# A fused spectral mixer and SwiGLU kernel: row scales stored from GpSimd, and transfers given other places in the order

## The chip, the cores and the metric

The kernel runs on one core of a Trainium2 chip. A core has five engines with a queue of its own each: TensorE (PE in the profile, with weight loads as PEld), VectorE (DVE), ScalarE (ACT), GpSimd (POOL) and SyncE (SP). Each works its queue strictly in order and waits where an instruction's input or buffer isn't ready. PE writes to PSUM banks, DVE and ACT read them. Transfers between HBM and SBUF are issued by SP or by GpSimd and carried out by DMA engines that they share. The metric is the device time of one execution in microseconds; lower is better.

## The reference, cut to what matters

There are 8 sequences of 3008 rows with 256 channels. Each is filtered in the frequency domain, and every row of the result then goes through an RMS norm and a SwiGLU feed-forward layer without biases.

```python
X = np.fft.rfft(x, axis=1)                       # x: 8 x 3008 x 256
Y = X * (filt_r + 1j * filt_i)[None]
y = np.fft.irfft(Y, n=3008, axis=1)              # -> 24064 rows of 256
rms = np.sqrt(np.mean(y * y, axis=-1, keepdims=True) + 1e-06)
xn = y / rms * rms_g
g = xn @ w_gate                                  # 256 x 1536
out = (g / (1 + np.exp(-g)) * (xn @ w_val)) @ w_out
```

## The kernel before

The transform of 3008 = 64 x 47 points is done as matmuls in four stages for each sequence. Stage A (`a_unit`, 12 a sequence) multiplies x by the 64-point table, copies the PSUM result to a tile `t1` on ACT or DVE, and stores each `t1` (3 units, a chunk) to the HBM buffer `z_tmp` (`z_store`). A bounce load (`t2_load`, 4 a sequence) brings it back in another order. Stage B (`b_unit`, 16 a sequence) does the second step, and multiplies by the filter (`s1`, `s2`). For sequences 2 to 7 this is done by DVE and a sum on GpSimd (`swap_unit`, L277); for sequence 1 the two products are made by DVE, or, for some units, by GpSimd, and then ACT first copies the PSUM bank to a tile `v`[...]. `v` is taken from the pool `yp`, which has three buffers and serves the norm's tiles `y` as well. `bi_unit` transforms back some slots later (a lag of 4 for sequence 1, 5 for sequence 2, 8 after that), `g_store` stores to `g_tmp`, `t4_load` brings it back, and `n_unit` does the last step and gives `y` and its squares. `negate` turns the sign of a quarter of the filter for the later sequences, on GpSimd, during stage B of sequence 1.

Sequence 0 has no other work to run beside. It stays on the chip through transposes, in a part ahead of the main loop; the filter, the weights (`w_load`, three parts) and x are loaded there.

The norm of a tile of 512 rows, called (b, m), takes: `q_unit`, a sum of squares on PE, `u` on DVE and the power -0.5 on GpSimd, which gives the row scales `rho`; `rho_move`, which stores `rho` to the HBM buffer `r_tmp` (2 KB); `rho_load`, which reads it back to all partitions as `rb` (256 KB, on SP); and `xn_unit`, the product of `y` and `rb` on GpSimd. The first two tiles of sequence 0 take another way, over PE (`scale_split`, `scale_apply`).

The main loop has 576 items (b, m, jt): 8 sequences, 6 tiles of rows, 12 blocks of 128 hidden columns. Item i does the gate and value matmuls (`gv`: `pg`, `pv`, L421), SiLU on ACT (L425), the product on DVE (L426), and two items later the output matmuls (`down`, L438). Everything else is put in by hand: `at(slot, fn, ...)` adds a call behind the item of that number, and the lists `a_at`, `b_at`, `n_at` and the offsets at L713 to L759 say which. The order of calls is the order on each engine. So a slot says behind what an instruction stands in its engine's queue, and not when it runs: a GpSimd or SP instruction starts as soon as all ahead of it on that queue are done and its own waits are over.

Three more things matter. GpSimd's transfers use eight semaphores in turn, so that one waits for the landing of the one eight before it; SP's likewise. Stage A uses PSUM bank 3 for units copied by DVE and bank 0 for those copied by ACT (`bank(3 if on_dve else 0, ...)`, L202); bank 3 is also stage B's and bank 0 that of `bi_unit` and `n_unit`. And `t1` has two buffers, so chunk c + 2 of stage A waits until chunk c has landed in `z_tmp`; x (`xp`) has four.

Of the kernel before, what the change touches and what calls it, by code (L numbers as in the profile page):

```python
# [20 lines left out]
P = 128  # L21
# [13 lines left out]
NXC = H // XC  # L35
# [87 lines left out]
def kernel(  # L123
# [11 lines left out]
    nc = tc.nc  # L135
# [7 lines left out]
    r_d = nc.dram_tensor("r_tmp", (B, 6, P * 4), FP32, kind="Internal").ap()  # L143
# [36 lines left out]
    def x_load(b, c):  # L180
        t = xp.tile([P, XC, D], FP16, tag="xc", name="xc")
        last = c == NXC - 1
        if last:
            nc.gpsimd.memset(t[64:P, XC - 1, :], 0.0)
        rows = x[b].rearrange("(n2 n1) d -> n2 n1 d", n1=N1)
        for h in range(2):
            w = XC - 1 if (last and h) else XC
            lo = h * H + c * XC
            nc.gpsimd.dma_start(t[h * 64:h * 64 + 64, 0:w, :], rows[:, lo:lo + w, :])  # L189
        st[b]["x"][c] = t  # L190

    def bank(i, name):

        pool, tag = ((psM, "mx"), (psG, "pg"), (psV, "pv"), (psB, "mb"), (psO, "po1"), (psO, "po0"))[i]
        return pool.tile([P, 512], FP32, tag=tag, name=name)
# [26 lines left out]
    def filt(k, n):  # L222
        c, r = divmod(k, KC)
        return fr[c][:, r:r + n, :], fi[c][:, r:r + n, :]
# [4 lines left out]
    def b_unit(b, i):  # L229
        if b:  # L230
            ps = bank(3, "psb")
        else:
            ps = bank((0, 3, 4, 5)[i % 4], "psb")
        ps = ps.rearrange("p (a d) -> p a d", a=2)
        for u in range(2):
            k = 2 * i + u
            if b:
                w, t = late_p["wb"], st[b]["t2"][k // KC][:, k % KC, :]
            else:
                w, t = wbp, st[0]["t2"][k // 4][:, k % 4, :]  # L240
            nc.tensor.matmul(ps[:, u, :], w[:, k, :], t, start=True, stop=True)  # L241
        f1, f2 = filt(2 * i, 2)
        if b:
            s1 = late_p["sp"].tile([P, 2, D], FP16, tag="s1", name="s1")
            s2 = late_p["sp"].tile([P, 2, D], FP16, tag="s2", name="s2")
            if b > 1:
                nc.vector.tensor_tensor(out=s1, in0=ps, in1=f1, op=ALU.mult)  # L247
                st[b]["s"][i] = (s1, s2, ps, f2)
                return
        elif i % 2:  # L250
            s1 = hp.tile([P, 512], FP16, tag="sg", name="sg").rearrange("p (a d) -> p a d", a=2)
            s2 = hhs[(i // 2) % 4].rearrange("p (a d) -> p a d", a=2)
        else:
            ss = xnp.tile([P, 2, 512], FP16, tag="xn", name="ss")
            s1, s2 = (ss[:, e, :].rearrange("p (a d) -> p a d", a=2) for e in range(2))
        eng = nc.vector
        if (i % 3 == 2) if b else (i in (4, 8, 11)):
            eng = nc.gpsimd
            v = yp.tile([P, 2, 512], FP32, tag="y", name="v")
            v = v[:, 0, :].rearrange("p (a d) -> p a d", a=2)  # L260
            nc.scalar.activation(out=v, in_=ps, func=AXT.Copy)
            ps = v
        eng.tensor_tensor(out=s1, in0=ps, in1=f1, op=ALU.mult)
        eng.tensor_tensor(out=s2, in0=ps, in1=f2, op=ALU.mult)  # L264
        st[b]["s"][i] = (s1, s2)
# [41 lines left out]
    def nq(b, m):  # L307
        return 3 if (m == 5 and b % 2 == 0) else 4
# [38 lines left out]

    def rho_move(b, m):
        n = nq(b, m)
        nc.sync.dma_start(r_d[b, m, 0:n * P].rearrange("(p q) -> p q", q=n),  # L350
                          st[b]["u"].pop(m)[:, 0:n])

    def rho_load(b, m):
# [122 lines left out]
    def f_dup(c):  # L476
        for t, a, e in ((fr[c], HALF, 0), (fi[c], 0, HALF)):
            if c == 2 or (c == 3 and a):
                nc.scalar.activation(out=t[a:a + HALF], in_=t[e:e + HALF], func=AXT.Copy)
            else:  # L480
                nc.gpsimd.tensor_copy(out=t[a:a + HALF], in_=t[e:e + HALF])
# [98 lines left out]
    def w_load(q):  # L580
        cols = ts(q, DFF // 3)
        for src, dst in ((moe_w_gate, wg), (moe_w_val, wv)):
            nc.gpsimd.dma_start(dst[:, :, cols], src.rearrange("(dt p) j -> p dt j", p=P)[:, :, cols])
        nc.gpsimd.dma_start(wo[:, ts(q, JT // 3), :],
                            moe_w_out.rearrange("(jt p) d -> p jt d", p=P)[:, ts(q, JT // 3), :])

    with tc.manual_schedule():
# [49 lines left out]
        for i in range(16):  # L637
            if i == 7:
                f_dup(3)
            b_unit(0, i)  # L640
            if i % 2 and i >= 5:
                bit_unit(i - 5)
                bit_unit(i - 4)
            if i == 4:
                f_dup(2)
            if i == 11:
                for q in range(3):
                    w_load(q)
                x_load(1, 0)
                x_load(1, 1)  # L650
        for i in range(12, 16):
            bit_unit(i)
        t2_unit(0, 1)
# [9 lines left out]
        scale_apply(0, 3)  # L663
        t2_unit(4, 0)
        t2_unit(5, 0)
        x_load(1, 2)
        x_load(1, 3)

        def open_late():
            nc.sync.dma_start(bass.AP(tensor=g_d.tensor, offset=g_d.offset + (H - 1) * D,  # L670
# [18 lines left out]
        def at(slot, fn, *a):  # L689
            todo = (late if fn == q_unit else plan).setdefault(slot, [])  # L690
            if fn in (sq_unit, swap_unit):
                todo.insert(0, (fn, a))
            else:
                todo.append((fn, a))

        def norm_plan(b, m, s0, s1, r):
            for dh in range(2):
                at((s0, s1)[dh], n_unit, b, m, dh)
                at((s0, s1)[dh] + 1, sq_unit, b, m, dh)
            for d, fn in zip(r, (q_unit, rho_move, rho_load, xn_unit)):  # L700
                at(s1 + d, fn, b, m)
# [11 lines left out]
        for b in range(1, B):  # L713
            t = (b - 1) * 72
            on_dve = ()
            n_at = [t + 51 + 8 * m for m in range(6)]
            n_step, lag, t4_at = 4, 8, t + 46
            a_at = [t - 103 + 12 * (i // 2) + 4 * (i % 2) for i in range(12)]
            b_at = [t - 26 + 4 * i for i in range(16)]
            if b == 1:  # L720
                a_at = [8, 9, 9, 10, 10, 11, 11, 12, 12, 13, 13, 14]
                on_dve = (2, 4, 6, 8, 10)
                b_at = [22 + 7 * i // 4 for i in range(16)]
                lag, t4_at = 4, 55
                n_at, n_step = [58, 62, 74, 86, 95, 107], 3
            elif b == 2:
                a_at = [51, 52, 53, 53, 54, 55, 55, 56, 56, 57, 57, 58]
                on_dve = (0, 2, 3, 5, 6, 8, 10, 11)
                b_at = [71 + 3 * i for i in range(16)]
                lag, t4_at = 5, 123  # L730
                n_at = [127 + 8 * m for m in range(6)]
            elif b == 3:
                a_at = [72, 73, 80, 81, 83, 84, 92, 93, 101, 102, 104, 105]
            for i in range(12):
                at(a_at[i], a_unit, b, i, i in on_dve)
                if i % 3 == 2:
                    at(a_at[i] + 1, z_store, b, i // 3)
            for c in range(4):
                at(b_at[0] - 4 + c // (1 + (b == 1)) if c < 3 else b_at[4] + 1, t2_load, b, c)
            for i in range(16):  # L740
                s0 = b_at[i]
                at(s0, b_unit, b, i)
                if b > 1:
                    at(s0 + 1, swap_unit, b, i, 0)
                    at(s0 + 2, swap_unit, b, i, 1)
                at(s0 + lag, bi_unit, b, i)
                if b == 1 and i in (3, 7, 11, 15):
                    at(s0 + 2, negate, i // 4, 0, 8)
                if i % 2 == 1:
                    at(s0 + lag + 1, g_store, b, i // 2)  # L750
            if b + 1 < B:
                for c in range(NXC):
                    at(a_at[3 * c + 2] + 2, x_load, b + 1, c)
            for c in range(4):
                at(t4_at + (c // 2 * 2 if b == 1 else c), t4_load, b, c)
            for m in range(6):
                step = 2 if b == 1 and m < 2 else n_step
                norm_plan(b, m, n_at[m], n_at[m] + step,
                          (2, 4, 6, 10) if b > 1 else (2, 3, 4, 7))  # L759
# [45 lines left out]
```

## Time and profile before

| | before |
|---|---|
| median of 8 runs | 939.6 us (937.61 to 945.3) |
| the profiled execution | 938.85 us, span 937.1 us |
| PE busy | 892.6 us (95%) |
| DVE, ACT, POOL busy | 673.6 (72%), 620.2 (66%), 390.4 us (42%) |
| mean granted TensorE clock | 0.979 |
| DMA moved | 101.17 MB, mean 108 GB/s |
| SP's queue | 34.3% of 16 engines' span |
| GpSimd's queue | 11.3% of 16 engines' span |

Times are in microseconds from the first instruction. "Busy" adds an engine's instructions; matmuls overlap one another, so that a busy PE may still be slower than it could be. In a group or a timeline row the engine, the source line, `out<-in` by the program's names and the shapes are given; what stands in brackets is the idle time just before and what ended it. A row of the waits reads: engine, line, what it waited for, microseconds in total, times, longest. `SPq` is SP issuing a transfer. The granted clock is 1.0 at full speed.

### The profile page before, as it was taken

The numbers are of one execution on the slowest core, as the hardware profiler recorded it, in microseconds if no ns is written. First come the engines' busy times: TensorE is split into PE (matmuls) and PEld (weight loads), VectorE is DVE, ScalarE is ACT, GpSimd is POOL, SyncE is SP. The second block draws the span as 40 slices with busy tenths as digits, with TensorE's granted clock in tenths as the row PEclk, the third lists the DMA queues.
The fourth block names the chain that finished last, engine by engine and source line by source line (L and its number), as shares of the span: only waits on it lengthen the run. The fifth ranks groups of instructions, "written<-read, shape, count | busy, mean of one in ns | idle before, by whom it ended". The sixth has DMA issues, their size and how long they took to land.

```text
span 937.1 us, 17504 instructions
## 1 busy us (share of the span) xinstructions
PE 892.6 (95%) x6321; PEld 564.1 (60%) x6321; DVE 673.6 (72%) x1068; ACT 620.2 (66%) x1049; POOL 390.4 (42%) x315
## 2 busy tenths in 40 slices
PE   8779898899989999999999999999999999999997
PEld 5555455556546666666666666666666666666554
DVE  7746456578878777787868778788878888555554
ACT  7647455567747776687667776687656775576543
POOL 7923486245532554145532554044522554033200
PEclk9779799999999999999999999999999999999999
DMA  8588433736536444643565434543353323332201
GB/s 200 88 154 188 90 83 79 205 88 146 131 98 168 96 97 113 184 97 98 96 187 116 97 83 112 171 94 83 80 172 82 64 63 71 100 71 49 57 24 45
DMA packets 85074, 101.17 MB, mean 108 GB/s; under 512 B 13296, under 2 KB 61616, under 8 KB 84604
## 3 DMA queue, kind: packets, MB, share of 16 engines
q1 hardware_dynamic: 76044, 83.81, 34.3%
q0 software_dynamic: 8944, 16.26, 11.3%
q8 instruction: 49, 0.80, 0.4%
q14 instruction: 37, 0.30, 0.1%
HBM read 67.93 MB, written 46.79 MB: 122 GB/s over the span
## 4 chain that ended last, share of the span: by engine, by line
PE 74%; DMA 10%; DVE 5%; POOL 4%; issue 2%; ACT 2%; SPq 1%; POOLq 0%; DVEq 0%; ACTq 0%
PE po L438 22%; PE pg L421 22%; PE pv L421 21%; PE psi L286 2%; PE psb L241 2%; DVE hh L426 2%; PE psn L318 2%; DMA fr<-in_filt_r_dram 2%; DMA t<-g_tmp 2%; PE psa L204 2%; DVE o L444 1%; DMA t<-z_tmp 1%; DMA z_tmp<-t 1%; DMA g_tmp<-t 1%; POOL xn L405 1%
## 5 line engine op out<-in xcount | busy, mean ns | idle before, releaser
L426 DVE TENSOR_TENSOR hh<-pv,sg 128x512 f16<-128x512 f32 (+1 forms) x576 | 391.7, 680 | 223.1 <-ACT sg L425 104.8
L425 ACT ACTIVATE sg<-pg 128x512 f16<-128x512 f32 (+1 forms) x576 | 338.9, 588 | 253.7 <-PE pg L421 243.4
L438 PE MATMUL po<-wo,hh 128*128 128x256 f16 x2256 | 346.3, 274 | 2.7 <-DVE o L444 0.6
L421 PE MATMUL pg<-xn,wg 128*128 128x512 f16 (+1 forms) x1152 | 340.5, 377 | 0.4 <-POOL xn L405 0.4
L421 PE MATMUL pv<-xn,wv 128*128 128x512 f16 (+1 forms) x1152 | 340.3, 377 | 0.0
L438 PEld LDWEIGHTS <-hh 128*128 128x128 f16 x2256 | 217.8, 98 | 106.9 <-issue 10.9
L277 POOL TENSOR_TENSOR s<-s,s 128x512 f16<-128x512 f16 x96 | 110.7, 1153 | 326.2 <-DVE s L274 254.8
L421 PEld LDWEIGHTS <-wv 128*128 128x128 f16 x1152 | 113.3, 98 | 133.1 <-issue 3.9
L405 POOL TENSOR_TENSOR xn<-y,rb 128x1024 f16<-128x1024 f32 (+1 forms) x46 | 128.9, 2803 | 60.9 <-DMA rb<-r_tmp 49.0
L274 DVE TENSOR_TENSOR s<-psb,fi 64x512 f16<-64x512 f32 x192 | 132.2, 688 | 5.9
L421 PEld LDWEIGHTS <-wg 128*128 128x128 f16 x1152 | 109.4, 98 | 13.7 <-issue 1.4
L345 POOL TENSOR_TENSOR rho<-u,mhalf 128x4 f32<-128x4 f32 (+1 forms) x48 | 48.5, 1011 | 73.3 <-DVE u L343 66.8
L291 ACT ACTIVATE t<-psi 96x512 f16<-96x512 f32 x112 | 66.4, 593 | 12.3 <-PE psi L286 7.3
L324 ACT ACTIVATE y<-psn,gsb 128x512 f32<-128x512 f32 (+1 forms) x94 | 63.8, 679 | 10.6 <-PE psn L318 3.9
L247 DVE TENSOR_TENSOR s<-psb,fr 128x512 f16<-128x512 f32 x96 | 65.3, 680 | 4.2 <-PE psb L241 4.2
L330 ACT ACTIVATE sq<-psn 128x512 f16<-128x512 f32 (+1 forms) x94 | 54.8, 582 | 0.0
L241 PE MATMUL psb<-t,wb 96*128 96x256 f16 x224 | 43.9, 277 | 11.3 <-DMA t<-z_tmp 9.3
L209 ACT ACTIVATE t<-psa 128x512 f16<-128x512 f32 x71 | 42.4, 597 | 10.4 <-PE psa L204 4.5
L286 PE MATMUL psi<-s,wi 128*128 128x256 f16 x248 | 46.0, 275 | 1.1 <-POOL s L264 1.0
L318 PEld LDWEIGHTS <-t 128*128 128x128 f16 x368 | 28.9, 99 | 22.9 <-issue 2.8
L286 PEld LDWEIGHTS <-wi 128*128 128x128 f16 x248 | 24.4, 99 | 27.3 <-issue 2.4
L189 POOL DMA_DIRECT2D xc<-in_x_dram x64 | 35.2, 555 | 13.1 <-PE psa L204 8.2
(96 smaller groups left out, 475.3 us busy)
## 6 DMA issues: line engine op xcount, KB each, us to landing
out_dram<-o SPq DMA_DIRECT2D x84, 256.0 KB
xc<-in_x_dram POOLq DMA_DIRECT2D x56, 192.0 KB, 6.3
rb<-r_tmp SPq DMA_DIRECT2D x42, 256.0 KB
z_tmp<-t SPq DMA_DIRECT2D x28, 384.0 KB
t<-z_tmp SPq DMA_DIRECT2D x28, 384.0 KB
g_tmp<-t SPq DMA_DIRECT2D x56, 192.0 KB
t<-g_tmp SPq DMA_DIRECT2D x21, 384.0 KB
out_dram<-o SPq DMA_DIRECT2D x12, 192.0 KB
```

The lines of the kernel that those rows point to most:

```text
L241: nc.tensor.matmul(ps[:, u, :], w[:, k, :], t, start=True, stop=True)
L247: nc.vector.tensor_tensor(out=s1, in0=ps, in1=f1, op=ALU.mult)
L274: nc.vector.tensor_tensor(out=s2[a], in0=ps[e], in1=f2[e], op=ALU.mult)
L277: nc.gpsimd.tensor_tensor(out=s, in0=s1, in1=s2, op=ALU.add)
L286: nc.tensor.matmul(ps[:, u, :], wi_at(q, 2 * i + u), ss[q][:, u, :], start=(q == 0), stop=(q == n - 1))
L291: nc.scalar.activation(out=st[b]["t3"][c][:, 2 * r:2 * r + 2, :], in_=ps[0:KR], func=AXT.Copy)
L324: nc.scalar.activation(out=y[:, dh, 0:w], in_=ps[:, 0:w], func=AXT.Identity, scale=gsb[:, dh:dh + 1])
L405: nc.gpsimd.tensor_tensor(out=xv, in0=yv, in1=rv.unsqueeze(1).to_broadcast([P, 2, n, P]), op=ALU.mult)
L421: nc.tensor.matmul(ps[:, 0:w], wt[:, dt_, ts(jt, P)], xn[:, dt_, 0:w], start=(dt_ == 0), stop=(dt_ == 1))
L425: nc.scalar.activation(out=sg[:, 0:w], in_=pg[:, 0:w], func=AXT.Silu)
L426: nc.vector.tensor_tensor(out=hh[:, 0:w], in0=pv[:, 0:w], in1=sg[:, 0:w], op=ALU.mult)
L438: nc.tensor.matmul(po[s4 // 2][:, s4 % 2, :], hh[:, ts(s4, P)], wo[:, jt, :], start=(jt == 0 and s4 % 2 == 0), stop=(jt == JT - 1 and (s4 ...
```

## The change

It moves calls, and changes four things that are more than a place:

- `rho_move` issues its store on GpSimd's queue instead of SP's. 46 stores are concerned.
- Of stage B of sequence 1, units 5, 8, 11 and 14 have their products made on GpSimd; unit 2 goes to DVE.
- In stage A of sequence 2 the units alternate so that no slot has two units on one PSUM bank; chunk 1 ends a slot earlier, the other three in the same slots.
- The bounce loads of sequences 2 to 7 have 7, 5 and 3 slots' lead for the first three, instead of 4, 3 and 2. For sequence 1 the leads are 5, 4 and 3 instead of 4, 4 and 3.

The other two are places alone: the last third of the weights and the first half of x of sequence 1 are issued behind the first row scale instead of ahead of it; and x of sequence 2 is called in slots 24 to 30 instead of 11 to 16, x of sequence 3 in slots 61 to 67 instead of 55 to 60. On GpSimd's queue the first chunk of x of sequence 3 then still stands ahead of the row scale of tile (1, 0), called in slot 62, and the other three behind it.

```diff
-        if (i % 3 == 2) if b else (i in (4, 8, 11)):
+        if (i in (5, 8, 11, 14)) if b else (i in (4, 8, 11)):
             eng = nc.gpsimd
...
     def rho_move(b, m):
         n = nq(b, m)
-        nc.sync.dma_start(r_d[b, m, 0:n * P].rearrange("(p q) -> p q", q=n),
+        nc.gpsimd.dma_start(r_d[b, m, 0:n * P].rearrange("(p q) -> p q", q=n),
                           st[b]["u"].pop(m)[:, 0:n])
...
             if i == 11:
-                for q in range(3):
-                    w_load(q)
-                x_load(1, 0)
-                x_load(1, 1)
+                w_load(0)
+                w_load(1)
...
         t2_unit(5, 0)
-        x_load(1, 2)
-        x_load(1, 3)
+        w_load(2)
+        for c in range(NXC):
+            x_load(1, c)
...
             elif b == 2:
-                a_at = [51, 52, 53, 53, 54, 55, 55, 56, 56, 57, 57, 58]
-                on_dve = (0, 2, 3, 5, 6, 8, 10, 11)
+                a_at = [51, 52, 53, 53, 54, 54, 55, 55, 56, 56, 57, 58]
+                on_dve = (0, 1, 3, 5, 7, 9, 10, 11)
...
             for c in range(4):
-                at(b_at[0] - 4 + c // (1 + (b == 1)) if c < 3 else b_at[4] + 1, t2_load, b, c)
+                at(b_at[0] - (5 if b == 1 else 7) + (1 if b == 1 else 2) * c if c < 3 else b_at[4] + 1,
+                   t2_load, b, c)
...
             if b + 1 < B:
                 for c in range(NXC):
-                    at(a_at[3 * c + 2] + 2, x_load, b + 1, c)
+                    at((24, 61)[b - 1] + 2 * c if b < 3 else a_at[3 * c + 2] + 2, x_load, b + 1, c)
```

## The prediction, made before the changed kernel had run

> **What bounds the kernel now.** I number the 576 items by the pairs of gate matmuls (`pg`, L421) in PE's timeline; item k starts slot k. First the window view, by stretches: before slot 0, slots 0 to 35, 36 to 52, 53 to 71, 72 to 119, 120 to the end. Columns: length, then busy time of PE, weight loads, DVE, ACT, POOL, then granted clock, DMA share, GB/s.
> ```profile
> 0.00:53.42 53.42, 38.40 (x430) 28.21 (x431) 37.69 (x64) 34.22 (x48) 43.99 (x56) 0.84 0.79 151
> 53.42:126.81 73.39, 65.35 (x442) 40.15 (x441) 39.99 (x71) 43.42 (x75) 31.43 (x26) 0.90 0.62 132
> 126.81:157.48 30.67, 29.17 (x196) 18.83 (x194) 19.99 (x31) 19.08 (x33) 23.48 (x9) 1.00 0.25 65
> 157.48:191.13 33.65, 27.12 (x188) 17.00 (x186) 16.86 (x30) 17.05 (x32) 9.41 (x12) 0.95 0.73 185
> 191.13:275.87 84.74, 79.24 (x525) 47.82 (x522) 67.73 (x105) 56.65 (x97) 41.11 (x34) 0.98 0.50 119
> 275.87:937.10 661.23, 653.27 (x4552) 412.04 (x4549) 491.30 (x771) 449.74 (x766) 241.01 (x179) 1.00 0.41 98
> ```
> From slot 120 on PE is busy 653.27 of 661.23 us at full clock: nothing that only removes waits gains there. All that can be won lies before 276 us. Second, PE's own waits:
> ```profile
> PE psb L241 <- DMA t<-z_tmp: 9.3, 3, 4.0
> PE psr L390 <- DVE hl L380: 5.2, 1, 5.2
> PE psa L204 <- DVE t L207: 2.7, 2, 1.4
> PE psi L286 <- ACT sq L330: 2.3, 1, 2.3
> PE psn L318 <- ACT t L209: 2.0, 1, 2.0
> ```
> Third, the timelines, to find what is behind each. POOL at the start: an x load waits for a landing, and the first row scale waits behind it, though DVE has given `u` at 45.76 (its row: 45.60, 0.16 long).
> ```profile
> 49.57 0.52 POOL L189 DMA_DIRECT2D xc<-in_x_dram  x1 [0.80 <-DMA wv<-in_moe_w_val_dram]
> 50.10 1.06 POOL L345 TENSOR_TENSOR rho<-u,mhalf 128x4 f32<-128x4 f32 x1
> ```
> ACT in slot 25: the copy of product i=2 for GpSimd waits for a `y` buffer, freed by `xn` of tile (0,3).
> ```profile
> 105.33 0.60 ACT L261 ACTIVATE v<-psb 128x512 f32<-128x512 f32 x1 [1.19 <-POOL xn L405]
> ```
> SP around slot 116: it holds the bounce loads of sequence 3 behind a store that waits for a row scale; PE then waits for them in slot 118.
> ```profile
> 262.60 0.33 SPq L350 DMA_DIRECT2D r_tmp<-rho  x1
> 264.03 0.33 SPq L356 DMA_DIRECT2D rb<-r_tmp  x1
> 264.46 0.94 SPq L219 DMA_DIRECT2D t<-z_tmp  x2
> ```
> The row of PE in slot 118 that waits for it:
> ```profile
> 272.29 0.61 PE L241 MATMUL psb<-t,wb 96*128 96x256 f16 x2 [3.48 <-DMA t<-z_tmp]
> ```
>
> **What the Trainium skill says.** "DMA: Bandwidth & Descriptors", Anatomy of one DMA: a GpSimd transfer has about 2.0 us fixed, and semaphore waits sit on the issuing sequencer. The trace agrees with the second: SP waits 246.5 us for `rho` at L350. The page's "Issuing engines are not separate DMA queues" says all share 16 engines; here the third `t<-z_tmp` issue took 4.11 us and its data came late while x loads moved. "TensorE: Matmul & The Clock Gate", Part 1: after an idle window of about 3.4 us PE runs at half clock until a busy one. The window view shows clock 0.50 from 46.9 to 57.1, 94.8 to 101.5, 108.4 to 111.7, 173.3 to 176.6 and 272.3 to 275.6, each after a wait. "PSUM — Partial Sum Buffer", summary of rules: read one bank while PE writes another; two `psa` users on one bank cost PE 1.36 us twice.
>
> **The change part by part.**
>
> *Weights and x of sequence 1.* Of these 17 issues 13 stood ahead of the first `rho`; now six do, and the last third of the weights and all of x come behind it. No work is added. POOL ends the six weight issues at 43.45, `rho` starts at 45.8 instead of 50.10: -4.3 us for `hl`, `psr`, slot 0. PE's gap shrinks from 5.25 to about 1 us, so full clock returns a window or so sooner: -1.0. The last weights landed 51.87 to 54.53; they follow the same queue, and are needed in slot 8 (about 62), x by slots 8 to 14 (lands by about 62). Cover of 7 us; each us beyond it would cost one. Sum **-5.3**.
>
> *x of sequence 2 behind slot 24, and product i=2 to DVE.* Six of its eight issues fell between 82.8 and 86.2 and held the DMA engines while the bounce loads stood in slot 22 (PE waited 4.00). Without them the last `z_tmp` store of stage A (82.09, less 5.3, landing in some 2.8 instead of 3.80) is down by 79.6, and the three bounce loads (1.15 MB; they moved in 5.5 us once the x loads were through) land from about 83 to 87: the first before slot 22's use at 86.3. Product i=2 leaves POOL (2 x 1.27) and ACT (0.60) for DVE (0.69 + 0.68; it idles over 1 us in most of these slots): the stall through slots 26 and 27 (4.2 and 3.8 us long instead of about 1.8) goes. Unhindered, slots 22 to 33 would take 20.3 us instead of 31.4, and slot 34 would start at 105.8 instead of 122.16. But slot 34 needs product i=5 from GpSimd, and there POOL's order decides: `rho` of tile 3 ends 84.1 (89.44 less 5.3); the store, which before shows only on SP, is bounded by SP's idle 1.4 in all from below and by GpSimd's slowest loads, 9.86, from above; I take 2.4 (0.6 issue, between an x load's 0.55 and a weight's 0.80, and landing at the skill's fixed price), 86.5; broadcast 3.7 (98.59 to 102.30), 90.3; `xn` 2.87; then the store of tile 4 (2.4), 95.6; its broadcast beside four x issues, 5.0 (rows: 3.4 to 5.5), 100.7; `xn` 2.87; a store 0.6, two x issues 1.1, the sign change 5.4, two products 2.5: 113.3. It was 124.48. So 11.2 us ahead, and PE waits 6 to 7 us in slot 34, which drops its clock: +2. At slot 48: 9 ahead, that is **-3.7** on top. With idle queues (broadcast 3.4, no clock drop) it is -7; with a store of 4 us landing, 0.
>
> *Stage A of sequence 2, x of sequence 3.* Slots 52 to 60 hold 7.8 us over their matmuls (52: 0.9; 53 and 55: 1.5 each; 58: 2.2; 59, 60 at half clock: 1.6). One user a bank removes the two 1.36 and a 0.68. The other: `z_tmp` store of chunk 1 took 6.40 with three x chunks in flight; their issues now stand on POOL behind the scale of slot 62, only the first stays. I take chunk 1's landing a slot earlier, and 1.7 us of wait left: **-6** (3 to 7).
>
> *Bounce loads of sequence 2 (slot 71).* They stood behind the second scale store (186.19); PE waited 1.77. They now go behind the first broadcast alone. But `xn` of tile (1,0) ended at 190.5, when slot 72 began at 191.1: its chain (store, broadcast, 2.87) is not shorter. **0** (-1.5 to +1.5).
>
> *Bounce loads of sequence 3 (slots 118, 119).* They go out after the output store at 256, about 257 instead of 264.46, needed at 268.9; with the 7.77 us that the late ones took they land at 265. The two slots took 5.98 + 2.33 instead of 1.5 each: **-5.3**.
>
> *46 stores on POOL.* At 0.55 each (x issue) 25 us, in the last stretch beside 241 of 661 busy; PE hides them. Queued behind: the stage B sums (L277), which PE wants only 8 slots after their unit (5 for sequence 2), and `xn`, seven slots early. Without that cover each would cost its 0.55. SP drops 46 issues, and waits at L356 for the landing instead of at L350.
>
> Sum: -5.3 - 3.7 - 6 + 0 - 5.3 = **-20.3**, from the profiled execution's 938.85 (span 937.1 plus 1.75 around it) to 918.5; the median of the runs shown is 0.75 above it, so **919**.
>
> **Rivals.** (a) *GpSimd's chain in slots 24 to 34 is shorter* (broadcasts as quick as the idle ones, no lost clock): 25 us gained, 914. For it: SP's queue is emptier there. Against: four x issues stand beside the second broadcast. (b) *The stores land slower, or stage A stays held by the landing of `z_tmp`*: 4 to 6 us landing costs 5 to 10, the other 4: 927. For it: GpSimd's loads took 3.45 to 9.86 us to land. Against: those moved 160 KB and more, a store 2 KB. (c) *Slower*: one mechanism, the landing of the GpSimd store. It counts twice in the chain to slot 34 and once for slot 72, 3 us for each us over 2.4; break-even at 2.4 + 20.3/3 = 9.2 us, and at 11 us the kernel takes about 945. Only the heaviest loads took so long. (d) *No change*: PE's idle comes back at the next limit, POOL being 23.48 of 30.67 us busy in slots 36 to 52; it would need the chain to take all of the first two parts and the DMA the rest: 939.
>
> **Chances.** Main case 0.42 (own range 916 to 923); (a) 0.25; (b) 0.25; (c) 0.05; (d) 0.03. A range of 910 to 931 takes in (a), the main case and most of (b), leaving out 2 in 10. About 0.3% (2.8 us) is what a measurement tells from no change: faster 0.92, within 0.03, slower 0.05.
>
> **What would show it.** Right: `psr` no longer waits 5 us, slot 0 near 49; slot 22 without a wait for `t<-z_tmp`; a wait of PE for `s` L264 in slot 34 of some 6 us; `psa` without waits for DVE; no DMA wait in slot 118; the stretch from slot 120 still 661 us. Wrong: an `r_tmp` store that lands later than 4 us, waits of PE for `xn`, or new gaps after slot 120, where POOL's sums would be late.

## The result: 5 us gained where 20 were forecast

The changed kernel takes 935.04 us (median of 12 runs, 933.38 to 937.35), the kernel before 940.24 us (33 runs). The ratio is 0.9945, 95% interval 0.993 to 0.996. The forecast was 919 us, range 910 to 931: the direction was right, the size was not.

The profiled execution has a span of 933.3 us (before 937.1) and a mean granted clock of 0.982 (0.979). The window view of the changed kernel, cut at the same slots as the one shown of before (0, 36, 53, 72, 120), with the same columns:

```profile
0.00:51.27 51.27, 38.92 (x429) 28.51 (x430) 37.82 (x64) 34.30 (x48) 40.60 (x50) 0.85 0.72 141
51.27:122.04 70.77, 62.08 (x442) 38.78 (x441) 40.73 (x73) 42.90 (x74) 35.39 (x35) 0.94 0.71 148
122.04:151.87 29.83, 29.02 (x197) 18.86 (x194) 19.84 (x32) 18.71 (x32) 22.86 (x9) 1.00 0.27 69
151.87:187.59 35.72, 25.76 (x189) 16.60 (x186) 16.94 (x30) 17.40 (x33) 10.86 (x15) 0.94 0.72 173
187.59:272.43 84.84, 78.56 (x523) 47.45 (x522) 67.21 (x105) 56.65 (x97) 41.43 (x37) 0.99 0.50 120
272.43:933.30 660.87, 653.34 (x4552) 411.96 (x4549) 491.51 (x771) 449.89 (x766) 264.89 (x217) 1.00 0.38 98
```

The last stretch is as long as before, 660.87 against 661.23, though GpSimd is busy 264.89 us in it instead of 241.01. The fourth, slots 53 to 71, became longer (35.72 against 33.65); no other grew by more than 0.1 us. Cut finer, by the prediction's own parts, from the starts of slots in both traces:

| part | forecast, us | before | after | change |
|---|---|---|---|---|
| start, to slot 8 | -5.3 | 68.04 | 65.19 | -2.9 |
| slots 8 to 50 | -3.7 | 85.13 | 83.21 | -1.9 |
| slots 51 to 60, stage A of sequence 2 | -6 | 24.02 | 20.88 | -3.1 |
| slots 61 to 117 | 0 | 90.37 | 98.47 | +8.1 |
| slots 118 and 119 | -5.3 | 8.31 | 4.68 | -3.6 |
| slot 120 to the end | 0 | 661.23 | 660.87 | -0.4 |
| sum | -20.3 | 937.1 | 933.3 | -3.8 |

Half of the miss is the row that was forecast at nothing. PE's waits in the changed kernel:

```profile
PE psi L286 <- POOL s L263: 6.0, 1, 6.0
PE psb L241 <- DMA t<-z_tmp: 5.7, 1, 5.7
PE psa L204 <- DVE t L207: 3.3, 1, 3.3
PE psi L286 <- POOL s L277: 3.1, 2, 2.6
PE psr L390 <- DVE hl L380: 1.0, 1, 1.0
```

Before, the list began with `t<-z_tmp` 9.3 in three waits and `psr` 5.2. `psr` is down to 1.0, and the bounce loads of slots 22 and 118 no longer appear. In their place stand four waits, in slots 34, 71, 57 and 76. Each is followed below.

**Slot 34** (10.08 us long instead of 3.35). GpSimd's timeline from the row scale of tile 3 of sequence 0 to product i=5, which slot 34 needs:

```profile
85.49 1.03 POOL L345 TENSOR_TENSOR rho<-u,mhalf 128x4 f32<-128x4 f32 x1 [6.27 <-DVE u L343]
86.81 0.64 POOL L350 DMA_DIRECT2D r_tmp<-rho  x1 [0.29 <-POOL rho L345]
92.99 1.03 POOL L345 TENSOR_TENSOR rho<-u,mhalf 128x4 f32<-128x4 f32 x1 [5.54 <-DVE u L343]
94.01 2.85 POOL L405 TENSOR_TENSOR xn<-y,rb 128x1024 f16<-128x1024 f32 x1
96.81 0.62 POOL L350 DMA_DIRECT2D r_tmp<-rho  x1
97.43 2.12 POOL L189 DMA_DIRECT2D xc<-in_x_dram  x4
100.79 0.88 POOL L345 TENSOR_TENSOR rho<-u,mhalf 128x3 f32<-128x3 f32 x1 [1.24 <-DVE u L343]
105.34 2.88 POOL L405 TENSOR_TENSOR xn<-y,rb 128x1024 f16<-128x1024 f32 x1 [3.68 <-DMA rb<-r_tmp]
108.17 0.64 POOL L350 DMA_DIRECT2D r_tmp<-rho  x1
108.81 1.07 POOL L189 DMA_DIRECT2D xc<-in_x_dram  x2
109.96 5.39 POOL L269 TENSOR_SCALAR fi<-fi 64x2048 f32<-64x2048 f32 x1
115.43 1.26 POOL L263 TENSOR_TENSOR s<-v,fr 128x512 f16<-128x512 f32 x1
116.66 1.26 POOL L264 TENSOR_TENSOR s<-v,fi 128x512 f16<-128x512 f32 x1
```

The scale of tile 4 is ready at 94.02, but its store stands behind `xn` of tile 3 and starts at 96.81, 2.8 us later. Then four x issues follow, and the broadcast goes out beside them, as SP's row shows:

```profile
98.63 0.34 SPq L356 DMA_DIRECT2D rb<-r_tmp  x1
```

It keeps `xn` of tile 4 waiting until 105.34. Product i=5 ends at 117.9, where the forecast had 113.3. PE runs at clock 0.51 from 114.8 to 121.7, during and after its wait.

**Slots 71 and 76.** SP's and GpSimd's timelines:

```profile
175.61 0.33 SPq L356 DMA_DIRECT2D rb<-r_tmp  x1
176.10 2.21 SPq L219 DMA_DIRECT2D t<-z_tmp  x2
189.29 0.34 SPq L356 DMA_DIRECT2D rb<-r_tmp  x1
```

```profile
174.41 2.10 POOL L189 DMA_DIRECT2D xc<-in_x_dram  x4
176.76 1.02 POOL L345 TENSOR_TENSOR rho<-u,mhalf 128x4 f32<-128x4 f32 x1 [0.25 <-DVE u L343]
182.38 2.85 POOL L405 TENSOR_TENSOR xn<-y,rb 128x1024 f16<-128x1024 f32 x1 [4.59 <-DMA rb<-r_tmp]
185.18 0.64 POOL L350 DMA_DIRECT2D r_tmp<-rho  x1
194.49 2.85 POOL L405 TENSOR_TENSOR xn<-y,rb 128x1024 f16<-128x1024 f32 x1 [7.33 <-DMA rb<-r_tmp]
```

Four x issues of sequence 3 leave GpSimd at 174.41 to 176.5, the two bounce loads leave SP from 176.10 on, among them. PE's first row with the bounced chunk:

```profile
186.57 0.59 PE L241 MATMUL psb<-t,wb 96*128 96x256 f16 x2 [5.66 <-DMA t<-z_tmp]
```

And of before, SP's issue of that load and PE's row:

```profile
186.19 0.32 SPq L219 DMA_DIRECT2D t<-z_tmp  x1
190.59 0.38 PE L241 MATMUL psb<-t,wb 96*128 96x256 f16 x2 [1.77 <-DMA t<-z_tmp]
```

From issue to use it is 10.5 us, where before it was 4.4; but there the load went out alone, the next one 3.5 us behind it, and here two go out together. PE waits 5.66 us in slot 71, and clock 0.50 from 183.1 to 189.9 makes it 7.50 + 2.57 for slots 71 and 72 instead of 3.13 + 1.41. Next, the scale of tile (1,1) is ready at 177.8, but its store has to wait for `xn` of tile (1,0), which waits for a broadcast beside the same x loads: 185.18, 7.4 us late. In both places store and `xn` are called in the same slot (24 and 67), `xn` first; the other order was not tried. So `xn` of (1,1) starts at 194.49, the sum `s` (L277) behind it is late, and slot 76 takes 4.31 us instead of 1.52.

**Slots 57 and 118.** In slot 57 the first copy of chunk 3 waits for `t1`, that is, for the landing of chunk 1 in `z_tmp` (SP's issues and DVE's row); in slot 118 PE's row no longer names a transfer, but the bank:

```profile
154.32 0.87 SPq L300 DMA_DIRECT2D t<-g_tmp  x2
156.26 0.33 SPq L215 DMA_DIRECT2D z_tmp<-t  x1
163.54 0.69 DVE L207 CAST t<-psa 128x512 f16<-128x512 f32 x1 [3.32 <-DMA z_tmp<-t]
```

```profile
270.48 0.38 PE L241 MATMUL psb<-t,wb 96*128 96x256 f16 x2 [1.48 <-DVE s L274]
```

**The store itself.** The 46 stores that GpSimd now issues:

```profile
L350 POOL DMA_DIRECT2D r_tmp<-rho x46: 612/618/644, 69.8 to 870.3; - x46
DMA to landing us min/median/max: 1.7/1.8/4.3
```

An issue holds GpSimd 0.62 us, and the store lands 1.8 us after the start of its issue in the median. "DMA: Bandwidth & Descriptors" of the Trainium skill, Anatomy of one DMA, has 2.0 us fixed for a GpSimd transfer; the measured 1.8 decides, and even the slowest, 4.3, is far from the 9.2 us at which the forecast's slower rival would have begun. From SP, in the kernel before, the same stores took 1.4 to 6.9 us from their issue to that of the broadcast that waits for them (median 2.0).

### The profile page after: what moved, and what is told of

It reads as the page before. It is cut to its first block, busy times and chain, and to the rows that moved or that the text cites. A ratio compares the mean times of both kernels' runs of the same rounds, so it can differ in the third digit from the quotient of the medians.

```text
span 933.3 us, 17516 instructions
## 1 busy us (share of the span) xinstructions
PE 887.7 (95%) x6321; PEld 562.1 (60%) x6321; DVE 674.1 (72%) x1070; ACT 619.8 (66%) x1048; POOL 416.0 (45%) x359
## 4 chain that ended last, share of the span: by engine, by line
PE 74%; DMA 9%; DVE 5%; POOL 4%; issue 4%; ACT 2%; SPq 1%; POOLq 0%; DVEq 0%; ACTq 0%
PE po L438 22%; PE pg L421 22%; PE pv L421 21%; DMA rb<-r_tmp 3%; DVE hh L426 2%; PE psi L286 2%; PE psb L241 2%; DMA fr<-in_filt_r_dram 2%; PE psn L318 2%; PE psa L204 2%; DVE o L444 1%; DMA r_tmp<-rho 1%; POOL xn L405 1%; DMA t<-g_tmp 1%; DVE s L274 1%
## 5 line engine op out<-in xcount | busy, mean ns | idle before, releaser
L438 PEld LDWEIGHTS <-hh 128*128 128x128 f16 x2256 | 217.1, 98 | 105.7 <-issue 10.1
L277 POOL TENSOR_TENSOR s<-s,s 128x512 f16<-128x512 f16 x96 | 110.6, 1153 | 291.5 <-DVE s L274 233.2
L405 POOL TENSOR_TENSOR xn<-y,rb 128x1024 f16<-128x1024 f32 (+1 forms) x46 | 128.7, 2798 | 66.8 <-DMA rb<-r_tmp 53.5
L291 ACT ACTIVATE t<-psi 96x512 f16<-96x512 f32 x112 | 66.4, 593 | 21.0 <-PE psi L286 16.1
```

The lines of the kernel that those rows point to most:

```text
L277: nc.gpsimd.tensor_tensor(out=s, in0=s1, in1=s2, op=ALU.add)
L291: nc.scalar.activation(out=st[b]["t3"][c][:, 2 * r:2 * r + 2, :], in_=ps[0:KR], func=AXT.Copy)
L405: nc.gpsimd.tensor_tensor(out=xv, in0=yv, in1=rv.unsqueeze(1).to_broadcast([P, 2, n, P]), op=ALU.mult)
L438: nc.tensor.matmul(po[s4 // 2][:, s4 % 2, :], hh[:, ts(s4, P)], wo[:, jt, :], start=(jt == 0 and s4 % 2 == 0), stop=(jt == JT - 1 and (s4 ...
```

## The experiments

The theory after this reading: two things that the forecast had at nothing took the gain. x loads on GpSimd, moved away from one transfer that PE waits for, stand beside another (slots 34 and 71). And a store on GpSimd is held by the compute instruction ahead of it, `xn` (slots 34 and 76). The rivals: the stores land late; the longer lead of the bounce loads itself costs in slot 71; or the gain was never there, each new wait only showing the next limit.

Lengths in us, from one profile of each; "34-40" is from the start of slot 34 to that of slot 41, and so on. Each ratio is to the runs of the kernel before that were taken beside that kernel. Rows up to "g_tmp loads later" are the changed kernel with one edit; the next three the kernel before with one edit; the last three the changed kernel with several.

| kernel | median | ratio to before, 95% | 22-27 | 34-40 | 55-58 | 71-72 | 76-89 | 118-119 |
|---|---|---|---|---|---|---|---|---|
| before | 940.24 | 1 | 21.3 | 13.9 | 10.7 | 4.5 | 23.7 | 8.3 |
| after | 935.04 | 0.9945 (0.993 to 0.996) | 11.7 | 21.5 | 11.3 | 10.1 | 26.2 | 4.7 |
| x of 3 spread | 934.44 | 0.9947 (0.9929 to 0.9965) | 11.7 | 21.5 | 12.0 | 5.4 | 28.2 | 4.7 |
| x of 3 early | 937.57 | 0.9986 (0.997 to 1.0002) | 11.7 | 21.3 | 17.3 | 6.7 | 25.3 | 4.7 |
| stores on SP | 930.24 | 0.9916 (0.989 to 0.9941) | 11.7 | 16.3 | 11.8 | 10.4 | 24.2 | 4.7 |
| x of 2 later | 929.96 | 0.9905 (0.9869 to 0.9941) | 11.7 | 18.7 | 12.3 | 9.8 | 26.5 | 4.7 |
| sign changes later | 930.23 | 0.9911 (0.9876 to 0.9946) | 11.7 | 22.0 | 7.9 | 9.9 | 25.2 | 4.7 |
| g_tmp loads later | 932.43 | 0.9931 (0.9905 to 0.9956) | 11.7 | 21.5 | 8.3 | 9.8 | 26.1 | 4.7 |
| before + leads | 938.13 | 0.9985 (0.9969 to 1.0002) | 18.9 | 14.3 | 10.2 | 5.3 | 24.8 | 4.7 |
| before + x of 2 | 934.74 | 0.9955 (0.9937 to 0.9974) | 15.5 | 16.1 | 10.1 | 4.3 | 23.7 | 7.7 |
| before + product i=2 | 934.54 | 0.9926 (0.9896 to 0.9956) | 14.5 | 14.3 | 12.7 | 4.8 | 23.9 | 7.9 |
| four moves, stores on GpSimd | 920.37 | 0.9776 (0.9746 to 0.9805) | 11.7 | 13.0 | 6.8 | 5.5 | 29.8 | 4.7 |
| four moves, stores on SP | 919.82 | 0.9797 (0.9766 to 0.9827) | 11.7 | 12.5 | 6.8 | 6.3 | 29.1 | 4.7 |
| the last, x of 3 wider | 917.63 | 0.9747 (0.9718 to 0.9776) | 11.7 | 12.5 | 6.9 | 5.6 | 25.8 | 4.7 |

A single profile's total also holds its own start, which varied by some 3 us among kernels with the same start code, so the verdicts below go by stretches. A stretch that ends on a transfer varies as well: slots 22 and 23 took 9.83 us before and 6.87 with product i=2 alone, an edit that changes nothing ahead of slot 25. So a difference of up to 3 us in one such stretch of one profile proves nothing by itself; the argument rests on larger ones and on those that several kernels repeat.

**Slot 71: is it the x loads?** First, x of sequence 3 spread over slots 61, 73, 80, 90:

```diff
-                    at((24, 61)[b - 1] + 2 * c if b < 3 else a_at[3 * c + 2] + 2, x_load, b + 1, c)
+                    at((24 + 2 * c, (61, 73, 80, 90)[c])[b - 1] if b < 3 else a_at[3 * c + 2] + 2, x_load, b + 1, c)
```

> The changed kernel, with chunks 1, 2 and 3 of x of sequence 3 called in slots 73, 80 and 90 instead of 63, 65 and 67 (chunk 0 stays). In the changed kernel PE waits 5.7 us in slot 71 for a bounce load that takes 10.4 us, and 2.6 us in slot 76 for a sum on GpSimd. Theory 1, the x loads hold the DMA engines while the bounce loads of sequence 2 stand in SP's ring: with the x loads gone from 174 to 187 us the bounce load lands in about 4.5 us, both waits go, about 8 us gained over the changed kernel, 927. Theory 2, the bounce load is late because it stands in SP's ring behind the 256 KB broadcast, itself held by the store on GpSimd: nothing changes, slot 71 keeps a wait of 5 us or more, 935.

Measured: slots 71 and 72 fall from 10.1 to 5.4 us, and no half clock follows. SP's issue and PE's row there:

```profile
176.75 0.90 SPq L219 DMA_DIRECT2D t<-z_tmp  x2
183.28 0.38 PE L241 MATMUL psb<-t,wb 96*128 96x256 f16 x2 [1.72 <-DMA t<-z_tmp]
```

So the x loads are the cause of the wait in slot 71: with nothing but them moved, the load takes 6.5 us to its use instead of 10.5. The 4.5 that I expected did not come: two bounce loads that go out together took 6 to 7 in every kernel here that has x elsewhere, and 10.1 to 10.5 in the four that leave it there with the stores on GpSimd. Of the 8 us expected little is left: slots 76 to 89 take back 2.0 (slot 76 waits 3.4 us for `s` L277), the profile as a whole is 2.0 us shorter, and the median hardly moves (934.44). Slot 76 has a cause of its own. Second, x of sequence 3 where the kernel before had it, ahead of the scale:

```diff
-                    at((24, 61)[b - 1] + 2 * c if b < 3 else a_at[3 * c + 2] + 2, x_load, b + 1, c)
+                    at(24 + 2 * c if b == 1 else a_at[3 * c + 2] + 2, x_load, b + 1, c)
```

> The changed kernel, with x of sequence 3 called where the kernel before has it, two slots behind its stage A chunk (55 to 60), so that its issues stand ahead of the row scale of slot 62. Theory 1: the waits in slots 71 and 76 go (8 us gained), and stage A of sequence 2 is longer than in the changed kernel by up to 3 us, since the x loads now share the engines with its stores: 927 to 930. Theory 2: slot 71 keeps its wait, 935 to 938.

Measured: slot 71 falls to 3.94 us here too (slot 72 runs at half clock, 2.72), yet slots 55 to 58 take 17.3 us instead of 11.3, 6 more where I expected up to 3: PE waits 7.1 us for DVE's copy in stage A, which waits for a `z_tmp` store that now runs beside the x loads. The collision has moved, not gone, and instead of the expected 927 to 930 the kernel is the slowest of the variants of the changed one (937.57). Third, the leads alone on the kernel before:

```diff
-                at(b_at[0] - 4 + c // (1 + (b == 1)) if c < 3 else b_at[4] + 1, t2_load, b, c)
+                at(b_at[0] - (5 if b == 1 else 7) + (1 if b == 1 else 2) * c if c < 3 else b_at[4] + 1,
+                   t2_load, b, c)
```

> The kernel before with the bounce loads' lead alone. The forecast's step for slots 118 and 119 gave 5.3 us; the changed kernel shows 3.6 there. Alone I expect those 3.6 us in slot 118, for the first two bounce loads of sequence 3 then stand ahead of the row scale store of slot 113 or so in SP's queue, and at slot 71 a wait no longer than the 1.8 us of before, since the x loads stand where they were: 935 to 936. If the store on SP still holds them, no change: 940.

Measured: slots 118 and 119 take 4.7 us, the whole of what the change gains there, and slots 71 and 72 take 5.3 instead of 4.5. The leads are not what costs 5.5 us in slots 71 and 72; they cost 0.8 there and 1.1 in slots 76 to 79 (both within the spread named above), where the store of tile (1,1), on SP, now takes 6.5 us behind the two bounce loads instead of 3.6 (to the issue of its broadcast). The expected 935 to 936 did not come, and the interval of the total (0.9969 to 1.0002) doesn't tell a gain from none.

**Slots 34 and 76: place in the queue or landing?** The stores back on SP, all else as changed:

```diff
-        nc.gpsimd.dma_start(r_d[b, m, 0:n * P].rearrange("(p q) -> p q", q=n),
+        nc.sync.dma_start(r_d[b, m, 0:n * P].rearrange("(p q) -> p q", q=n),
```

> The changed kernel with the row scales stored from SP again, all else as changed. Theory 1 (the x loads): slot 71 keeps a wait of 4 us or more, for the x loads still stand behind the row scale of slot 62; in the slots up to 34 the second store no longer stands behind xn on GpSimd, so the wait in slot 34 is shorter by 2 to 5 us; 930 to 935. Theory 2 (the store on GpSimd): the wait in slot 71 goes, and the time falls to 927 or so, or, if SP then holds the loads of sequence 3 again, 931.

Measured: slot 34 takes 4.92 us instead of 10.08, slot 76 is back at 1.52, slot 71 stays (7.66), though by another way: on SP the 2 KB store of tile (1,0) takes 4.9 us beside the x loads (171.00 to the broadcast's issue at 175.89), and the bounce loads stand behind both. GpSimd and SP in slots 24 to 34:

```profile
94.63 1.01 POOL L345 TENSOR_TENSOR rho<-u,mhalf 128x4 f32<-128x4 f32 x1 [6.42 <-DVE u L343]
95.61 2.88 POOL L405 TENSOR_TENSOR xn<-y,rb 128x1024 f16<-128x1024 f32 x1
98.44 2.17 POOL L189 DMA_DIRECT2D xc<-in_x_dram  x4
102.44 0.88 POOL L345 TENSOR_TENSOR rho<-u,mhalf 128x3 f32<-128x3 f32 x1 [1.82 <-DMA rb<-r_tmp]
103.30 2.86 POOL L405 TENSOR_TENSOR xn<-y,rb 128x1024 f16<-128x1024 f32 x1
```

```profile
95.67 0.32 SPq L350 DMA_DIRECT2D r_tmp<-rho  x1
97.11 0.32 SPq L356 DMA_DIRECT2D rb<-r_tmp  x1
```

The store goes out at 95.67, while GpSimd begins `xn`; the broadcast starts 1.44 us later, ahead of the x issues of 98.44, and `xn` of tile 4 begins 8.7 us after the start of the scale of tile 4 instead of 12.4 (92.99 to 105.34). Of these 3.7 us 3.2 are the earlier issue of the broadcast: 2.5 us after that start instead of 5.6. On GpSimd the store stands behind the 2.85 us of `xn`, and the broadcast behind that and beside the x loads. Since this store takes 1.8 us on GpSimd and 1.44 here, the landing is not what differs by 5 us: its place is. For slot 76 the case is weaker: two other kernels with the stores on SP, "before + leads" and the last of the table, have 2.85 and 3.00 there, so whether 1.3 or all of its 2.8 us are the store's is not settled. Next, the two other things in that chain, each by itself: x of sequence 2 in slots 37, 39, 43, 45, and the sign changes in slots 42, 48, 49, 51, stores still on GpSimd:

```diff
-                    at((24, 61)[b - 1] + 2 * c if b < 3 else a_at[3 * c + 2] + 2, x_load, b + 1, c)
+                    at(((37, 39, 43, 45)[c], 61 + 2 * c)[b - 1] if b < 3 else a_at[3 * c + 2] + 2, x_load, b + 1, c)
```

> The changed kernel with x of sequence 2 called in slots 37, 39, 43 and 45 instead of 24 to 30, so that none of its issues stands on GpSimd's queue ahead of product i=5. In the changed kernel slot 34 takes 10.1 us, since that product ends at 117.9. Theory, GpSimd's order decides there, with the second broadcast held by the x loads (6.7 us instead of 3.7) and 3.3 us of x issues in the chain: slot 34 takes 4 to 5 us, 5 to 6 less. Rival, the chain is set by the sign change and the stores alone: 1 to 3 less.

```diff
-                    at(s0 + 2, negate, i // 4, 0, 8)
+                    at((42, 48, 49, 51)[i // 4], negate, i // 4, 0, 8)
```

> The changed kernel with the four sign changes of the filter called in slots 42, 48, 49 and 51 instead of 29, 36, 43 and 50, behind the products that GpSimd makes. Theory, the 5.4 us of the first sign change stand whole in the chain to slot 34: slot 34 takes about 5 us instead of 10.1, and PE's clock does not drop after it. It may come back later: the sign changes then stand ahead of x of sequence 3 and of the scale of slot 62. Rival, slot 34 waits for something else: no change there.

Measured, x later: slot 34 takes 6.52 us, and `xn` of tile 4 waits 1.23 us for its broadcast instead of 3.68, though its store is issued as late as before. That is 3.6 us less, between the 5 to 6 of the theory and the 1 to 3 of its rival; the late store and the sign change are left. Measured, sign changes later: slot 34 takes 3.64 us, but slots 36 to 40 take 17.01 instead of 9.23, so that slots 34 to 40 together gain nothing (22.0 against 21.5). PE's new wait there, and GpSimd's row of `xn` of tile 5:

```profile
PE psb L241 <- ACT v L261: 5.5, 1, 5.5
```

```profile
116.36 1.99 POOL L405 TENSOR_TENSOR xn<-y,rb 128x768 f16<-128x768 f32 x1 [3.78 <-DMA rb<-r_tmp]
```

The copy `v` of the next product on GpSimd needs a `y` buffer that this `xn` frees, and its broadcast is late. The time of this run fell by 5 us all the same; the profile shows 3.5 of it in slots 55 to 58 and 1.1 in slots 76 to 89, which was no part of the reasoning and stays unexplained.

**Slot 57: the loads of g_tmp ahead of the store?** SP has two loads of `g_tmp`, 384 KB each, ahead of the chunk-1 store. Called one slot later:

```diff
-                lag, t4_at = 4, 55
+                lag, t4_at = 4, 56
```

> The changed kernel with the loads from g_tmp of sequence 1 called one slot later (56 and 58), so that the store of chunk 1 of stage A stands ahead of the first two in SP's queue. In the changed kernel that store takes 7.2 us to land, and slot 57 5.0 us. Theory, it waits behind 768 KB of loads in SP's ring: it lands in 3 to 4 us and slot 57 takes 2 us, 3 less; the first norm unit of slot 58 may then wait up to 1 us for its load. Rival, the x load of chunk 0 on the same engines holds it: no change in slot 57.

Measured: slot 57 takes 1.75 us instead of 5.01, and the three kernels below that have this edit among others take 1.6. In the changed kernel the store was issued at 156.26 and landed at 163.4, 7.2 us; here it is issued at 157.07, and the copy that waits for it starts without a wait, so that it had landed within 4.2 us:

```profile
161.29 0.69 DVE L207 CAST t<-psa 128x512 f16<-128x512 f32 x1
```

PE no longer waits for DVE there.

**Which edit removes what in slots 22 to 27?** Each alone on the kernel before:

```diff
-                    at(a_at[3 * c + 2] + 2, x_load, b + 1, c)
+                    at(24 + 2 * c if b == 1 else a_at[3 * c + 2] + 2, x_load, b + 1, c)
```

> The kernel before, with one change: x of sequence 2 called in slots 24 to 30 instead of 11 to 16. Theory (the x loads hold the DMA engines while the first bounce loads of sequence 1 stand in slot 22): slots 22 to 24 fall from 9.8 us to about 4.1, without a DMA wait of PE for t<-z_tmp; slots 26 to 28 keep their 7 to 8 us, since the copy v of product i=2 still waits for a y buffer. Rival 1 (the wait of slot 22 was the late z_tmp store or the lead of the loads): slots 22 to 24 stay above 8 us. Rival 2 (the stall of slots 26 to 28 was only the late start of the chain): they fall to about 4.7 as well. Total in either case near 937 to 940, for what is gained here can come back in slot 34.

```diff
-        if (i % 3 == 2) if b else (i in (4, 8, 11)):
+        if (i in (5, 8, 11, 14)) if b else (i in (4, 8, 11)):
```

> The kernel before, with one change: the products of stage B of sequence 1 made on GpSimd are units 5, 8, 11, 14, and unit 2 goes to DVE. Theory: slots 26 to 28 fall from 8.0 us to about 4.7, slots 22 to 24 stay near 9.8. Rival: slots 26 to 28 stay above 7 us, because what ended them was the late bounce loads and not the buffer of v. In both cases GpSimd reaches product i=5 no sooner than before, so that slot 34 takes back what is gained: total 938 to 941.

Measured: x of sequence 2 alone takes slots 22 and 23 from 9.83 to 4.08 us and leaves 26 and 27 at 8.44; product i=2 alone takes 26 and 27 from 7.98 to 4.64 and leaves 22 and 23 at 6.87 (the 3 us below the 9.83 of before are not its doing, as said). Both attributions hold. The totals I had expected do not: both are near 934.6, because slots 34 to 40 take back 2.2 us in one and 0.5 in the other, and not all. With i=2 gone GpSimd is free of its 2.54 us and ends product i=5 60.6 us after slot 2 began; before it was 66.8, and in the changed kernel, where both edits stand with the stores, 63.2. Up to slot 36, counted from slot 2, product i=2 alone gains 6.2 us and the whole change 1.8.

**All together.** The changed kernel with x of sequence 2 in slots 37 to 45, x of sequence 3 in 61, 73, 80, 90, the sign changes and the loads of `g_tmp` later, and the stores on SP (the other three lines as in the diffs above):

```diff
-                    at((24, 61)[b - 1] + 2 * c if b < 3 else a_at[3 * c + 2] + 2, x_load, b + 1, c)
+                    at(((37, 39, 43, 45)[c], (61, 73, 80, 90)[c])[b - 1] if b < 3 else a_at[3 * c + 2] + 2, x_load, b + 1, c)
```

> The changed kernel with the row scales stored from SP, the sign changes in slots 42, 48, 49 and 51, x of sequence 2 in slots 37 to 45, x of sequence 3 in 61, 73, 80 and 90, and the loads from g_tmp one slot later. If each wait is independent: slot 34 3 us less than with the SP store alone (4.9), slot 71 3.6 less, slot 57 3 less, some 10 us under that run: about 920. If the waits share one limit, the gain of one comes back in the next and it stays at 927 or above.

The same with the stores left on GpSimd, as the changed kernel has them:

```diff
-        nc.sync.dma_start(r_d[b, m, 0:n * P].rearrange("(p q) -> p q", q=n),
+        nc.gpsimd.dma_start(r_d[b, m, 0:n * P].rearrange("(p q) -> p q", q=n),
```

> The changed kernel with four moves and its stores left on GpSimd: sign changes in slots 42, 48, 49, 51; x of sequence 2 in slots 37, 39, 43, 45; x of sequence 3 in slots 61, 73, 80, 90; loads of g_tmp one slot later. It differs from the run of 919.8 us only in the queue of the 46 stores. Theory (a store on GpSimd costs by its place in that queue, behind xn): 924 to 928, with slots 34 to 41 some 3 to 8 us longer than the 12.5 us that they have with the store on SP, and slot 76 above 3 us instead of 1.53. Rival (with the x loads and sign changes out of the way the place costs nothing): 919 to 922, slots 34 to 41 and 76 as with the store on SP.

Measured: 919.82 and 920.37, the same within their intervals. With the store on SP slots 34, 71 and 57 take 1.96, 3.92 and 1.57 us, 3.0, 3.7 and 2.9 less than with the SP store alone: these waits were independent, and the expected 920 came. Slots 34 to 40 take 12.5 and 13.0 us: once the x issues and the sign changes are away from that chain, a store that waits 2.8 us behind `xn` costs nothing there. So the 5 us of the stores in slot 34 were the price of that place in that chain, and my expectation of 924 to 928 failed. In slots 76 to 79 it does cost: 11.8 against 6.8 us, with `xn` of tile (1,1) waiting 6.29 us for its broadcast. That the totals agree comes from slots 80 to 89, where the run with the stores on SP loses 22.3 us against 18.0. SP's rows there:

```profile
186.77 0.33 SPq L350 DMA_DIRECT2D r_tmp<-rho  x1
187.19 1.09 SPq L294 DMA_DIRECT2D g_tmp<-t  x1
191.52 0.32 SPq L356 DMA_DIRECT2D rb<-r_tmp  x1
```

The broadcast waits 4.75 us for the landing of its store, beside x issues of 186.72; on GpSimd, ahead of the same x issues, that store took 1.9. The tile is (1,2), not (1,1) as the expectation below has it. Last, the two later x chunks moved from slots 80 and 90 to 84 and 95:

```diff
-(61, 73, 80, 90)[c]
+(61, 73, 84, 95)[c]
```

> The kernel of the 919.8 us run (store on SP, sign changes and x of sequence 2 later, loads of g_tmp one slot later) with the last two x chunks of sequence 3 in slots 84 and 95 instead of 80 and 90. Theory: the scale store of tile (1,1), which took 4.75 us to land beside those x loads, lands in about 2.5, rb and xn come 2 us or more sooner, and slots 88 and 89 (5.28 and 3.41 us) return to about 2 us each: 915 to 917. Rival (slot 88 waits for the sum s for another reason, such as GpSimd's share of work): 919 to 921, slots 80 to 90 still near 22 us.

```profile
187.03 0.33 SPq L350 DMA_DIRECT2D r_tmp<-rho  x1
187.44 1.03 SPq L294 DMA_DIRECT2D g_tmp<-t  x1
189.27 0.32 SPq L356 DMA_DIRECT2D rb<-r_tmp  x1
```

Measured: 2.24 us instead of 4.75, slots 80 to 89 back at 18.0, and 917.63 us, ratio 0.9747 (0.9718 to 0.9776). It beats both kernels. That this is close to what the forecast gave the change itself is chance: it took four more moves, and the stores back on SP.

## Why the prediction was wrong

- **"Weights and x of sequence 1", -5.3: right, somewhat too large.** `psr` waits 1.0 us, the gap that was forecast. The pair of profiles shows -2.9 at slot 8, but the start varies: over all profiles slot 8 begins at 64.9 us on average with the new start (10 kernels, 63.2 to 66.8) and at 68.95 with the old (4 kernels, 68.0 to 70.5), so about -4.1. No run had this edit alone.
- **"x of sequence 2 behind slot 24, and product i=2 to DVE", -3.7: mechanism right, the chain mis-sized.** Of the 11.1 us of slots 8 to 33 9.6 came (slots 26 and 27 kept 1 us of their stall), and the wait in slot 34 came as well (6.0; forecast 6 to 7). Counted from slot 8, the forecast had product i=5 after 50.6 us (113.3 less 62.7); it ended after 52.7. The scale of tile 3 was on time to 0.1 us (21.3 against 21.4). The failed term is the "broadcast beside four x issues, 5.0", which took 6.7 (98.63 to 105.34); the rows of 3.4 to 5.5 that it was taken from leave out one of 6.6 in the trace of before, issued at 264.03. The rest is two smaller errors of opposite sign: `xn` of tile 3, which stood behind the scale of tile 4, ended 1.2 us later than forecast, and the store of tile 4 took 1.8 to the broadcast's issue instead of 2.4 (whose parts, as the forecast named them, make 2.6). The store of tile 4 behind `xn` was in that sum, but nothing set it against the store on SP, which runs beside `xn`: so the forecast took the chain's length for given, and did not see that one part of the change was eating another's gain.
- **"Stage A of sequence 2, x of sequence 3", -6: half right.** One user a bank did its part, as far as the traces of the whole change show (no run had it alone): PE's two waits of 1.36 are gone, and slots 51 to 54 take 6.9 us instead of 9.1, as the rule of "PSUM — Partial Sum Buffer" of the Trainium skill (summary of rules: read one bank while PE writes another) lets expect. The other half failed: I took "1.7 us of wait left" for the landing of chunk 1; it was 3.3, because taking x out of the way left the two loads of `g_tmp` ahead of the store, which the forecast did not name. With them behind it the wait was gone.
- **"Bounce loads of sequence 2 (slot 71)", 0 (-1.5 to +1.5): wrong, +5.5 in slots 71 and 72.** This is the step that failed most. It priced the loads' place on SP and forgot what the same change had put beside them: x of sequence 3 behind the scale of slot 62, that is, at the very time. I had read this effect in the trace of before in slot 22 and used it there as a gain. "DMA: Bandwidth & Descriptors", Issuing engines are not separate DMA queues, says that the transfers of all issuing engines run on the same 16 DMA engines and interleave; 10.5 against 6.5 us for the first load, with x alone moved, agrees with it.
- **"Bounce loads of sequence 3", -5.3: right, -3.6.** The transfers are in time. What remains in slot 118 is a wait of 1.48 us for the bank of stage B, hidden behind the DMA wait before. I took 1.5 us for each slot and did not ask what was late next.
- **"46 stores on POOL", hidden: wrong up to slot 80, right after slot 120.** I counted the 0.55 us that an issue holds back others, and named what queues behind it. I did not price what it is queued behind: `xn`. In the changed kernel this costs 5.2 us in slot 34 and 1.3 to 2.8 in slot 76; for the latter the step on slot 71 had looked at the chain of tile (1,0) only, not at that of (1,1) behind it.
- **The rivals.** (b), 927, named stage A held by `z_tmp`, rightly, and slower landings, wrongly; (c)'s landing of over 9.2 us is refuted by 1.8 (4.3 at most), and its yardstick was short: GpSimd's slowest load before took 10.9 us, not 9.86; (d) described the outcome best, "PE's idle comes back at the next limit", though the limit was not GpSimd's load in slots 36 to 52, and four moves of calls lifted it by another 15 us.
- **Open.** Why slots 26 and 27 with x of sequence 2 alone are 0.5 us longer than before, why the kernel with later sign changes gained in slots 55 to 58, and what makes slot 76 differ by 1.5 us among kernels with the stores on SP.

## What to carry to other kernels

When a transfer is moved, write down for its new place every load and store that PE will wait for in the next 10 us or so, as long as the slowed load took here: the relief at the old place and the collision at the new one are the same effect, and both have to be in the sum. When a store is moved to a compute engine's queue, price what stands ahead of it there, not only its own issue; whether that costs depends on how tight the chain behind it is. And a wait that is removed uncovers the one behind it: look for it in the same slot before giving the whole wait as a gain.

## What the runs showed of the hardware

- A 2 KB store from GpSimd to HBM landed 1.8 us after the start of its issue in the median (1.7 to 4.3 over 46), so GpSimd is not slow at storing; 0.62 us of it are spent on the engine. From SP it took 1.4 to 6.9 (median 2.0).
- Transfers issued on SP were slowed much beside x loads issued on GpSimd. In three pairs of kernels that differ in the places of x loads alone, a 384 KB load took 10.5 instead of 6.5 us until PE used it, a 256 KB broadcast 6.7 instead of 4.3 until `xn` began, and a 2 KB store 4.75 instead of 2.24 until the broadcast behind it went out.
- Each of PE's two longest waits in the changed kernel cost more than itself: in the waits of slots 34 and 71 (6.0 and 5.7 us) and behind them the granted clock was 0.51 and 0.50 for 6.9 and 6.8 us, and the following slots took 2.20 and 2.57 us instead of 1.30 and 1.41. "TensorE: Matmul & The Clock Gate", Part 1, of the Trainium skill has it so: half clock after an idle window of about 3.4 us, until a busy one.
